# Attention and a gated dense stage on one core: from hand-ordered heads and units per batch to a task graph over 512-token chunks ordered by a list scheduler

## The chip, the cores and the metric

The kernel runs on one core of a Trainium2 chip. The metric is device time in microseconds (us) of one execution; a lower figure is better. The profile is one execution, read with the engines PE (matmul; PEld is its weight load), ACT (activation functions), DVE (vector), POOL (GpSimd, which also issues DMAs that change the type) and SP (which issues plain DMAs).

## The reference

There are 4 batches, 8 heads, 768 tokens and a head size of 64. Heads 0, 2 and 6 attend causally to everything ("retrieval" heads); the other five ("streaming" heads) attend to the first 4 tokens and to a window of 64. The 8 heads side by side make 3072 rows `x` of 512 numbers, and a gated dense stage follows.

```python
scores = scale * np.matmul(q, k.transpose(0, 1, 3, 2))
scores = np.where(mask, scores, -1e9)          # causal, or causal & (sink | window)
a = np.exp(scores - max); a = a / sum(a)
x = np.matmul(a, v)                            # -> (3072, 512)

g = x @ w_gate                                 # 512 -> 1536
gelu = 0.5 * g * (1.0 + erf(g / sqrt(2)))
val = x @ w_val                                # 512 -> 1536
ffn_out = gelu * val @ w_out                   # 1536 -> 512
res_gate = sigmoid(x @ w_res)
return x + res_gate * ffn_out
```

## The kernel before, in words

**Attention by head.** For each of the 32 (batch, head) pairs POOL issues three loads, q, k and v, each of a whole head (`qk_dma`, lines 364 and 367; `v_dma`, line 374). They turn float32 into float16 on the way. SP then transposes q and k by DMA (`qk_transposes`, lines 382 and 387) from 64 columns padded to 128, into `QT` and `KT`. Four slots (`NSLOT`) hold heads in flight. A head is worked in three pairs of 128-query tiles. A pair's scores (line 421, 256 columns per matmul) go to one of two PSUM banks; the exponential (line 438, or 433 with a bias that leaves only the sink columns) takes them to `ET`; masks are multiplied in on DVE (line 448); the product with v and a column of ones (line 463) gives 65 columns per tile, of which the last is the sum. A reciprocal (line 475) and a scaling (line 480) write `xtok` in float32.

**Dense stage by batch.** When the 8 heads of a batch are done, `x_transposes` turns `xtok` with float32 transposes on PE (line 506) and 24 copies on DVE (line 513) into `xT`. Then come 24 gate-and-value units (12 feature groups for 512 tokens, 12 for the other 256): line 550 is the gate matmul, 560 the value matmul, 569 a Tanh on ACT that stands for the error function, 573 and 577 two DVE operations that make `hT`. Six output units follow: line 597 is `hT` by `wo`, 607 `xT` by `wr`, 615 a Tanh, 619 and 624 the gating and the residual on DVE. SP stores the rows at the start of the next batch's flush (line 630).

**What sets the order.** Every engine has one queue, in program order. The main loop writes it by hand: scores of a pair, one pending dense unit, the product with v of the pair before, another dense unit. A batch's dense stage therefore lies beside the next batch's attention, batch 0's attention has no dense work beside it, and the last dense stage has no attention beside it. `flush_batch` runs between two batches. Weights are issued on POOL two chunks per head, between the loads of q, k and v (lines 292 to 306). Each task waits on the semaphores of its readers and writers (`Sched.task`).

Of the kernel before, what the change touches and what calls it, by code (L numbers as in the profile page):

```python
# [1 line left out]

# [3 lines left out]
BATCH = 4  # L7
NHEAD = 8
# [7 lines left out]

NEG = -4000.0
SM_SCALE = 1.0 / 8.0
GELU_SIG = 1.702
# [3 lines left out]

ACT_EXP = mybir.ActivationFunctionType.Exp
ACT_TANH = mybir.ActivationFunctionType.Tanh
ACT_COPY = mybir.ActivationFunctionType.Copy

ALU_MUL = mybir.AluOpType.mult
ALU_ADD = mybir.AluOpType.add
ALU_GE = mybir.AluOpType.is_ge  # L30
ALU_NE = mybir.AluOpType.not_equal


class _Token:
    __slots__ = ("sem", "val")

    def __init__(self, sem, val):
        self.sem = sem
        self.val = val


class Sched:

    ENGS = ("pe", "act", "dve", "pool", "sp")

    def __init__(self, nc):
        self.nc = nc
        self.sems = {}
        self.counts = {}
        self.prog = {e: [] for e in self.ENGS}  # L50
        self.res_writer = {}
        self.res_readers = {}
        for e in self.ENGS:
            self.sems[e] = nc.alloc_semaphore(f"cnt_{e}")
            self.counts[e] = 0
        self.dma_sems = {}
        self.dma_counts = {}

    def _collect(self, waits, reads, writes):
        for r in reads:  # L60
            w = self.res_writer.get(r)
            if w is not None:
                waits.append(w)
        for r in writes:
            w = self.res_writer.get(r)
            if w is not None:
                waits.append(w)
            for t in self.res_readers.get(r, ()):
                waits.append(t)

    def _register(self, tok, reads, writes):
        for r in reads:
            self.res_readers.setdefault(r, []).append(tok)
        for r in writes:
            self.res_writer[r] = tok
            self.res_readers[r] = []

    @staticmethod
    def _dedupe(waits):
        wd = {}  # L80
        for t in waits:
            if t is None:
                continue
            key = id(t.sem)
            cur = wd.get(key)
            if cur is None or cur[1] < t.val:
                wd[key] = (t.sem, t.val)
        return list(wd.values())

    def task(self, eng, fn, waits=(), reads=(), writes=()):  # L90
        waits = list(waits)
        self._collect(waits, reads, writes)
        wlist = self._dedupe(waits)
        self.counts[eng] += 1
        tok = _Token(self.sems[eng], self.counts[eng])
        self.prog[eng].append((fn, wlist, tok, "inst"))
        self._register(tok, reads, writes)
        return tok

    def dma(self, eng, fn, sem_name, waits=(), reads=(), writes=()):  # L100
        waits = list(waits)
        self._collect(waits, reads, writes)
        wlist = self._dedupe(waits)
        if sem_name not in self.dma_sems:
            self.dma_sems[sem_name] = self.nc.alloc_semaphore(f"dma_{sem_name}")
            self.dma_counts[sem_name] = 0
        self.dma_counts[sem_name] += 16
        tok = _Token(self.dma_sems[sem_name], self.dma_counts[sem_name])
        self.prog[eng].append((fn, wlist, tok, "dma"))
        self._register(tok, reads, writes)  # L110
        return tok

    def group_register(self, tokens, reads=(), writes=()):
        for r in reads:
            self.res_readers.setdefault(r, []).extend(tokens)
        for w in writes:
            self.res_writer[w] = tokens[-1]
            self.res_readers[w] = []

    def emit(self, eng_name, engine):  # L120
        for fn, wlist, tok, kind in self.prog[eng_name]:
            for sem, val in wlist:
                engine.wait_ge(sem, val)
            res = fn(engine)
            insts = list(res) if isinstance(res, (list, tuple)) else [res]
            last = insts[-1]
            if kind == "dma":
                last.then_inc(tok.sem, 16)
            else:
                last.then_inc(tok.sem, 1)  # L130

    def final_waits(self, engine):
        for name, sem in self.dma_sems.items():
            v = self.dma_counts[name]
            if v > 0:
                engine.wait_ge(sem, v)


def build_kernel(
    nc,  # L140
    q, k, v, moe_w_gate, moe_w_val, moe_w_out, moe_w_res, out,
    *,
    batch=BATCH, nhead=NHEAD, seq=SEQ, dhead=DHEAD,
    n_sink=N_SINK, window=WINDOW, is_retrieval=IS_RETRIEVAL,
    d_ff=D_FF,
    moe_units_per_pair=2,
    debug=None,
):
    assert dhead == 64
    d_model = nhead * dhead  # L150
    assert d_model % 128 == 0 and d_ff % 128 == 0 and seq % 128 == 0
    nt = seq // 128
    assert nt % 2 == 0
    npairs = nt // 2
    ncb = d_model // 128
    nf = d_ff // 128
    assert window == 64 and 0 < n_sink <= 4

    S = Sched(nc)

    _static_seen = set()

    def sres(*names):
        out_ = []
        for n_ in names:
            if n_ not in _static_seen:
                _static_seen.add(n_)
                out_.append(n_)
        return out_

    def sba(name, shape, dt):
        return nc.alloc_sbuf_tensor(name, list(shape), dt)

    ident32 = sba("ident32", [128, 128], FP32)
    mk_causal_l = sba("mk_causal_l", [128, 256], FP16)
    mk_causal_r = sba("mk_causal_r", [128, 256], FP16)
    mk_sink0 = sba("mk_sink0", [128, 256], FP16)
    mk_bandr = sba("mk_bandr", [128, 256], FP16)
    mk_offl = sba("mk_offl", [128, 256], FP16)
    mk_bandoff = sba("mk_bandoff", [128, 256], FP16)  # L180
    sinkbias = sba("sinkbias", [128, 1], FP32)

    NSLOT = 4
    qst = [sba(f"qst{i}", [128, nt, 128], FP16) for i in range(NSLOT)]
    kst = [sba(f"kst{i}", [128, nt, 128], FP16) for i in range(NSLOT)]
    vaug = [sba(f"vaug{i}", [128, nt, dhead + 1], FP16) for i in range(NSLOT)]
    QT = [sba(f"QT{i}", [128, seq], FP16) for i in range(NSLOT)]
    KT = [sba(f"KT{i}", [128, seq], FP16) for i in range(NSLOT)]
    ET = [sba(f"ET{i}", [128, nt * 256], FP16) for i in range(2)]
    rcp = [sba(f"rcp{i}", [128, 2], FP32) for i in range(2)]  # L190
    xtok = [sba(f"xtok{i}", [128, nt, d_model], FP32) for i in range(2)]
    xT = [sba(f"xT{i}", [128, ncb, seq], FP16) for i in range(2)]

    wg = sba("wg", [128, ncb, d_ff], FP16)
    wv = sba("wv", [128, ncb, d_ff], FP16)
    wo = sba("wo", [128, nf, d_model], FP16)
    wr = sba("wr", [128, ncb, d_model], FP16)

    ssig = [sba(f"ssig{i}", [128, 512], FP16) for i in range(2)]
    usb = [sba(f"usb{i}", [128, 512], FP16) for i in range(2)]  # L200
    hT = sba("hT", [128, nf, seq], FP16)
    srs = [sba(f"srs{i}", [128, 512], FP16) for i in range(2)]
    msb = [sba(f"msb{i}", [128, 512], FP32) for i in range(2)]
    otile = [sba(f"otile{i}", [128, 512], FP32) for i in range(2 * nt)]
    deferred_out = deque()

    PB = [nc.alloc_psum_tensor(f"pb{i}", [128, 512], FP32) for i in range(8)]
    sunit = [PB[0], PB[1]]
    pavs = [PB[2], PB[3]]
    gpss = [PB[4], PB[6]]  # L210
    vpss = [PB[5], PB[7]]
    pffs = [PB[4], PB[6]]
    prss = [PB[5], PB[7]]

    def pool_chain(res, fns):
        tok = None
        for fn in fns:
            tok = S.task("pool", fn, reads=[res], writes=[res])
        return tok

    def aff(out, op, fill, base, pattern, cm):
        return lambda e: e.affine_select(out=out, in_=out, compare_op=op, fill=fill,
                                          base=base, pattern=pattern,
                                          channel_multiplier=cm)

    def build_consts():
        pool_chain("ident32", [lambda e: e.memset(ident32[:, :], 0.0),
                               aff(ident32[:, :], ALU_NE, 1.0, 0, [[-1, 128]], 1)])
        def q0(t):
            return t[:, 0:128]  # L230

        def q1(t):
# [543 lines left out]
```

## Time and profile before

| what | value |
|---|---|
| median of 3 runs | 428.47 us (428.27, 428.47, 431.46) |
| profiled execution: span from the first to the last instruction | 427.9 us |
| profiled execution: its own time | not listed apart from the span; the span lies 0.6 us under the median of the runs |
| mean granted TensorE clock in the profile | 0.950 |
| PE busy | 341.5 us (80%), 2144 matmuls |
| DVE busy | 268.7 us (63%), 856 instructions |
| ACT busy | 166.6 us (39%), 333 instructions |
| POOL busy | 103.2 us (24%), 158 instructions |
| moved by DMA | 34.05 MB in 138471 packets; read from HBM 29.36 MB, written 6.29 MB |

How to read it: a busy share is an average over stages. PE's records overlap, because a matmul's record holds its whole way through the array, so the pitch (start to start) is what a matmul costs in a row. A table of stretches (busy time of each engine between two moments) and the chain of work that ended last (each step with what released it) show the stages apart.

### The profile page before, as it was taken

How to read it: one execution, taken by the hardware profiler on the slowest of the kernel's cores; microseconds unless marked ns; L12 is line 12 of the kernel's file. 1: busy time of each engine (PE TensorE's matmuls, PEld its weight loads, DVE VectorE, ACT ScalarE, POOL GpSimd, SP SyncE). 2: the span in 40 equal slices, each digit the busy share in tenths (PEclk: the TensorE clock that was granted, in tenths of full speed). 3: DMA queues.
4: the chain of work that ended last, by engine and by line, in shares of the span. 5: the costliest groups of instructions: out<-in, count | busy, mean ns of one | idle time of the engine just before them, and what ended most of it. 6: DMA issues, size and time to landing. Idle time of an engine off the chain costs nothing.

```text
span 427.9 us, 7653 instructions
## 1 busy us (share of the span) xinstructions
PE 341.5 (80%) x2144; PEld 189.9 (44%) x2144; DVE 268.7 (63%) x856; ACT 166.6 (39%) x333; POOL 103.2 (24%) x158
## 2 busy tenths in 40 slices
PE   0176743898987896899987896899987896899995
PEld 0043321544575443544565443444564443445742
DVE  0065533767888356767887357778886447778643
ACT  1155632145555226144555216244555215133311
POOL 9895744221224003210224022120200000000000
PEclk9999999999999999599999999599999997699999
DMA  8999999999977509925578419944551110000021
GB/s 59 158 147 126 170 163 134 119 134 105 116 95 83 51 12 89 218 40 63 49 70 89 56 9 89 207 53 51 57 57 9 51 74 27 0 2 0 2 75 74
DMA packets 138471, 34.05 MB, mean 80 GB/s; under 512 B 127168, under 2 KB 135360, under 8 KB 138432
## 3 DMA queue, kind: packets, MB, share of 16 engines
q0 software_dynamic: 83776, 14.69, 52.7%
q1 hardware_dynamic: 54656, 18.88, 28.6%
q8 instruction: 20, 0.33, 0.3%
q14 instruction: 19, 0.16, 0.1%
HBM read 29.36 MB, written 6.29 MB: 83 GB/s over the span
## 4 chain that ended last, share of the span: by engine, by line
PE 62%; DMA 10%; DVE 9%; ACT 7%; issue 6%; DVEq 0%; SPq 0%; ACTq 0%
PE pb L597 15%; PE pb L550 14%; PE pb L560 13%; PE pb L421 7%; DMA KT<-kst 6%; PE pb L463 5%; PE pb L607 5%; DMA kst<-in_k_dram 4%; DVE xT L513 4%; ACT ET L438 4%; ACT ET L433 3%; PE pb L506 2%; DVE ET L448 2%; DVE usb L573 1%; DVE xtok L480 1%
## 5 line engine op out<-in xcount | busy, mean ns | idle before, releaser
L438 ACT ACTIVATE ET<-pb 128x512 f16<-128x512 f32 (+1 forms) x172 | 91.3, 546 | 89.2 <-PE pb L421 77.1
L421 PE MATMUL pb<-QT,KT 128*128 128x256 f16 x344 | 77.0, 318 | 54.5 <-DMA KT<-kst 27.7
L550 PE MATMUL pb<-xT,wg 128*128 128x256 f16 (+1 forms) x384 | 81.3, 335 | 0.0
L569 ACT ACTIVATE ssig<-pb 128x512 f16<-128x512 f32 (+1 forms) x96 | 47.0, 490 | 83.5 <-PE pb L550 73.2
L560 PE MATMUL pb<-xT,wv 128*128 128x256 f16 (+1 forms) x384 | 78.3, 326 | 0.0
L374 POOL DMA_DIRECT2D vaug<-in_v_dram x32 | 26.7, 834 | 185.8 <-PE pb L463 77.7
L463 PE MATMUL pb<-vaug,ET 128*128 128x65 f16 x552 | 53.4, 208 | 21.6 <-DVE ET L448 8.4
L421 PEld LDWEIGHTS pb<-QT,KT 128*128 128x128 f16 x344 | 29.2, 104 | 83.5 <-issue 46.9
L597 PE MATMUL pb<-wo,hT 128*128 128x512 f16 x288 | 66.0, 379 | 0.0
L573 DVE SCALAR_TENSOR_TENSOR usb<-ssig,pb 128x512 f16<-128x512 f16 (+1 forms) x96 | 52.9, 551 | 15.4 <-ACT ssig L569 5.6
L463 PEld LDWEIGHTS pb<-vaug,ET 128*128 128x128 f16 x552 | 36.1, 105 | 49.6 <-issue 14.3
L577 DVE SCALAR_TENSOR_TENSOR hT<-usb,pb 128x512 f16<-128x512 f16 (+1 forms) x96 | 53.2, 554 | 3.3
L480 DVE TENSOR_SCALAR xtok<-pb,rcp 128x64 f32<-128x64 f32 x192 | 45.8, 280 | 10.5 <-PE pb L421 0.2
L619 DVE SCALAR_TENSOR_TENSOR msb<-srs,pb 128x512 f32<-128x512 f16 x24 | 16.5, 687 | 54.1 <-PE pb L463 26.6
L560 PEld LDWEIGHTS pb<-xT,wv 128*128 128x128 f16 x384 | 37.8, 99 | 26.3 <-issue 1.3
L550 PEld LDWEIGHTS pb<-xT,wg 128*128 128x128 f16 x384 | 35.7, 99 | 18.3 <-issue 2.2
L615 ACT ACTIVATE srs<-pb 128x512 f16<-128x512 f32 x24 | 14.3, 597 | 73.2 <-PE pb L607 64.5
L597 PEld LDWEIGHTS pb<-wo,hT 128*128 128x128 f16 x288 | 27.4, 97 | 30.0 <-DVE xtok L480 0.2
L448 DVE TENSOR_TENSOR ET<-ET,mk_causal_l 128x256 f16<-128x256 f16 x36 | 10.4, 289 | 41.0 <-POOLq L271 21.4
L364 POOL DMA_DIRECT2D qst<-in_q_dram x32 | 27.0, 845 | 30.1 <-DMA KT<-kst 30.1
L513 DVE CAST xT<-pb 128x128 f16<-128x128 f32 x96 | 26.1, 290 | 8.2 <-PE pb L506 0.4
L506 PE MATMUL pb<-ident,xtok 128*128 128x128 f32 x96 | 26.4, 434 | 5.7 <-DVE xT L513 5.3
(43 smaller groups left out, 212.9 us busy)
## 6 DMA issues: line engine op xcount, KB each, us to landing
out_dram<-otile SPq DMA_DIRECT2D x24, 256.0 KB, 2.4
qst<-in_q_dram POOLq DMA_DIRECT2D x32, 96.0 KB, 5.0
kst<-in_k_dram POOLq DMA_DIRECT2D x32, 96.0 KB, 5.3
vaug<-in_v_dram POOLq DMA_DIRECT2D x32, 96.0 KB, 3.5
wg<-in_moe_w_gate_dram POOLq DMA_DIRECT2D x6, 256.0 KB, 8.3
wv<-in_moe_w_val_dram POOLq DMA_DIRECT2D x6, 256.0 KB, 18.4
wo<-in_moe_w_out_dram POOLq DMA_DIRECT2D x4, 384.0 KB, 30.1
QT<-qst SPq DMA_TRANSPOSE x32, 3.9
```

The costliest lines, as they stand in the source:

```text
L421: return [e.matmul(bank[:, slot * 256: slot * 256 + 256], lhsT=KT[sl][:, kt * 128:(kt + 1) * 128], rhs=QT[sl][:, 256 * p:256 * p + 256], s ...
L438: exp_fn = (lambda bank=bank, r0=r0, nblk=nblk: lambda e: e.activation(out=ET[eb][:, r0 * 256:(r0 + nblk) * 256], in_=bank[:, 0:nblk * 256 ...
L463: return [e.matmul(pav[:, dq * 128: dq * 128 + dhead + 1], lhsT=ET[eb][:, rank[kt] * 256 + dq * 128: rank[kt] * 256 + dq * 128 + 128], rhs ...
L480: S.task("dve", (lambda dq=dq, qt=qt: lambda e: e.tensor_scalar(out=xtok[xb][:, qt, h * dhead:(h + 1) * dhead], in0=pav[:, dq * 128: dq * ...
L506: return [e.transpose(out=tpav[:, cb * 128:(cb + 1) * 128], in_=xtok[xb][:, tt, cb * 128:(cb + 1) * 128], identity=ident32[:, :]) for cb i ...
L513: S.task("dve", (lambda tt=tt, cb=cb, tpav=tpav: lambda e: e.tensor_copy(out=xT[xb][:, cb, tt * 128:(tt + 1) * 128], in_=tpav[:, cb * 128: ...
L550: return [e.matmul(gps[:, 0:n], lhsT=wg[:, ci, f * 128:(f + 1) * 128], rhs=xT[xb][:, ci, c0:c0 + n], start=(ci == 0), stop=(ci == ncb - 1) ...
L560: return [e.matmul(vps[:, 0:n], lhsT=wv[:, ci, f * 128:(f + 1) * 128], rhs=xT[xb][:, ci, c0:c0 + n], start=(ci == 0), stop=(ci == ncb - 1) ...
L569: S.task("act", (lambda fb=fb, gps=gps: lambda e: e.activation(out=ssig[fb][:, 0:n], in_=gps[:, 0:n], func=ACT_TANH, scale=0.5 * GELU_SIG))(),
L573: S.task("dve", (lambda fb=fb, gps=gps: lambda e: e.scalar_tensor_tensor(out=usb[fb][:, 0:n], in0=ssig[fb][:, 0:n], scalar=1.0, in1=gps[:, ...
L577: S.task("dve", (lambda fb=fb, vps=vps: lambda e: e.scalar_tensor_tensor(out=hT[:, f, c0:c0 + n], in0=usb[fb][:, 0:n], scalar=0.5, in1=vps ...
L597: return [e.matmul(pff[:, 0:d_model], lhsT=hT[:, fi, tt * 128:(tt + 1) * 128], rhs=wo[:, fi, 0:d_model], start=(fi == 0), stop=(fi == nf - 1))
```

## The change

The whole program is rewritten. `Sched`, the main loop and its helpers go; a class `Graph` takes tasks with an estimated duration, a priority, dependencies and buffers, and `schedule()` puts each engine's queue in order at build time: at every moment a free engine takes the ready task with the lowest priority number whose buffers are free. `assign_waits()` then drops the waits that follow from others.

- Tokens are cut into six chunks of 512, which cross batch borders: `CHUNKS` has (batch, first tile, last tile) segments of 2 or 4 query tiles.
- q and k of a segment are loaded for all 8 heads by one DMA each (three groups of heads in the first chunk). A partition takes `n` neighbouring tokens, so that one run is `n`*64 numbers. A DVE copy (`rp`) puts two heads side by side, PE transposes them in float16 (`qkT`), and ACT (two of the first chunk's on DVE) copies them out of PSUM (`qkE`). The DMA transposes go.
- Scores are 128 columns per block and only for blocks that the masks leave; blocks are packed up to 512 columns for one exponential. The four sink columns are copied into the previous tile's block of k and v (`ks`, `ksf`, `vs`, `vsf`), which saves the sink block of its own.
- One reciprocal and one scaling per head and segment; `x` is copied to float16 (`x16`) and transposed in float16 (`xT`).
- The Tanh and the DVE operation after it give way to one Gelu on ACT. Exponentials of chunk c wait in ACT's order until the last Gelu of chunk c-1 has run; scores of chunk c wait for the transposes of `x` of chunk c-1.
- The residual is added on POOL (on DVE in the last chunk) and each tile is stored at once by SP.

The diff, cut to its core:

```diff
+CHUNKS = (((0, 0, 4),), ((0, 4, 6), (1, 0, 2)), ((1, 2, 6),),
+          ((2, 0, 4),), ((2, 4, 6), (3, 0, 2)), ((3, 2, 6),))
...
+    P_er = Pool(many("er", 3, [128, 2304], FP16))
+    P_es = Pool(many("es", 4, [128, 1024], FP16))
+    P_av = Pool(banks[0:2])
+    P_ps = Pool(banks[2:8], caps={"moe": 4, "scr": 3})
...
+    t_causal = chain(-40, [ ... 2 operations of 512 columns ])
+    t_diag = chain(-41, [ ... 4 operations, 3 of them of 640 columns ])
+    t_prev = chain(-40, [ ... 3 operations of 512 columns ])
...
+    def load_weights():
+        for j in range(3):
+            for nm, t, src in (("g", wg, w_gate), ("v", wv, w_val)):
+                wtok[nm, j] = dma("pool", -20 + j, 3.1, ...)
+        wtok["r"] = dma("pool", -12, 3.1, ...)
+        for j in range(4):
+            wtok["o", j] = dma("pool", -11 + j, 2.3, ...)
...
+        base = {0: -60, 1: -15}.get(c, 1000 * (c - 2) + 50)
+        groups = ((0, 2), (2, 4), (4, 8)) if c == 0 else ((0, 8),)
...  # q and k: one DMA a group; v: one DMA a head for batches 0 and 1, two a batch after that
+            tt = G.add("pe", c_mm(128, 2 * n), tr, [t_ident, tokr], pr, bufs=[rp, scr], name="qkT")
+            on = "dve" if c == 0 and p % 2 == 0 else "act"
...
+                ts = G.add("pe", ..., sc, deps, pr, bufs=[scr, ...], order=chunk_xt[c - 1], name=f"sc{h}")
+                tx = G.add("act", c_act(cols), ... func=AF.Exp ..., [ts], pr, bufs=[scr, et],
+                           fset="exp", order=[last_gelu[c - 1]], name=f"exp{h}")
+                    tm = G.add("dve", c_dve(w * 128, 2, False), ... ALU.mult ..., [tx, mt], pr, name=f"mask{h}")
...
+    def gate_value(c, xtbuf, xttoks):
+        for f in range(NF):
+            pr = 1000 * c + 500 + f
+            tg = G.add("pe", c_mm(512, NCB), mk(wg, gb), xttoks + [wtok["g", f // 4]], pr, bufs=[gb, xtbuf])
+            tv = G.add("pe", c_mm(512, NCB), mk(wv, vb), xttoks + [wtok["v", f // 4]], pr, bufs=[vb, xtbuf])
+            ta = G.add("act", c_act(512), ... func=AF.Gelu ..., [tg], pr, bufs=[gb, ga], fset="gelu")
+            th = G.add("dve", c_dve(512), ... scalar_tensor_tensor(in0=gact, scalar=0.5, in1=value bank) ...)
...
+    def output(c, h, htoks, xbuf, xtoks, xtbuf, xttoks):
+        for lt in range(4):
+            pr = 1000 * c + 1600 + 10 * lt
+            tr = G.add("pe", c_mm(512, NCB), ... wr ..., name="res")
+            for j in range(4):
+                prev_t = G.add("pe", c_mm(512, 3), ... wo ..., name="ff")
+            ta = G.add("act", c_act(512), ... func=AF.Tanh, scale=0.5 ..., name="tanh")
+            t1 = G.add("dve", c_dve(512), ... (tanh + 1) * ff ..., name="gated")
+            t2 = G.add("dve" if last chunk else "pool", ..., tensor_tensor add of x, name="add")
+            dma("sp", pr, ..., name="out")
...
-    (Sched, pair_scores_exp_mask, pair_av, x_transposes, moe_units, qk_dma, v_dma, qk_transposes and the main loop)
```

Attention of chunk c has the priorities 1000c to 1000c+240, gate and value 1000c+500 and up, output 1000c+1600 and up: the output of a chunk ranks behind both the attention and the gate stage of the next one.

More of the change, by code (lines that the diff above doesn't have):

```diff
@@ new lines, with __init__, can, take @@
+class Buf:
+    __slots__ = ("pool", "kind", "slot", "left", "users", "war", "free_at")
+    def __init__(self, pool, kind=None):
+        self.pool, self.kind = pool, kind
+        self.slot = None
+        self.left = 0
+        self.users = []
+        self.war = []
+        self.free_at = 0.0
+class Pool:
+    def __init__(self, items, caps=None):
+        self.items = items
+        self.caps = caps or {}
+        self.held = {}
+        self.free = [(0.0, i) for i in range(len(items))]
+        self.last = [[] for _ in items]
+    def can(self, kind, t):
+        if kind in self.caps:
+            h = self.held.get(kind, [])
+            h[:] = [f for f in h if f is None or f > t]
+            if len(h) >= self.caps[kind]:
+                return False
+        return any(f <= t for f, _ in self.free)
+    def take(self, buf, t):
+        best = min(x for x in self.free if x[0] <= t)
+        self.free.remove(best)
+        buf.slot = best[1]
+        buf.war = list(self.last[best[1]])
+        self.held.setdefault(buf.kind, []).append(None)
+    def give(self, buf, t):
+        h = self.held[buf.kind]
+        h.remove(None)
+        h.append(t)
+        self.free.append((t, buf.slot))
+        self.last[buf.slot] = list(buf.users)
```

1204 lines of the change are left out of this document (592 added, 612 removed).

## The prediction

> **What bounds the kernel now.** I read the chain of work that ended last first, then stretches of the span between its turning points, then the groups by shape, then the timeline where a pitch was needed. The chain's rows are start, length (us), what.
>
> ```profile
> span 427.9 us, 7653 instructions
> ...
> by line: DMA KT<-kst 27.6%; DMA kst<-in_k_dram 20.8%; PE pb L421 5.9%; DVE xT L513 4.9%; PE pb L463 2.9%; issue 2.7%; PE pb L506 2.3%; PE pb L550 2.1%; ACT ET L438 2.0%; SPq L382 1.5%; DVE ET L448 1.3%; PE pb L560 1.0%; DVE xtok L480 0.6%;
> ...
> 29.43 13.20 DMA KT<-kst
> 44.15 18.72 DMA kst<-in_k_dram
> 62.94 11.60 DMA KT<-kst
> 86.87 1.68 PE pb L550 x4
> 88.55 0.86 PE pb L560 x4
> ...
> 182.40 1.70 PE pb L550 x4
> ...
> 277.70 1.71 PE pb L550 x4
> ...
> 370.52 1.51 PE pb L550 x4
> ...
> 402.56 2.59 PE pb L597 x12
> ...
> 422.42 0.88 PE pb L607 x4
> ```
>
> The row "by line" covers the first 90 us alone. Three parts follow. Up to 86.9 us DMA carries the chain (loads of k and the DMA transposes, 48% of those 90 us) and no dense matmul runs. Then come three periods of 95.5, 95.3 and 92.8 us (from the starts at 86.87, 182.40, 277.70 and 370.52), in which PE leads. From 370.5 to 423.3 the last dense stage runs alone: it holds 192 matmuls of 512 columns at 0.2155 us (2.59/12, and 0.86/4) and 96 of 256 at half of that, 51.9 us, and takes 52.8: 98%. PE can thus run almost dense.
>
> The periods can't. Busy time per stretch, with the granted clock:
>
> ```profile
> core 0: us, PE busy (x) PEld busy (x) DVE busy (x) ACT busy (x) POOL busy (x), PEclk, DMA share, GB/s
> 87.00:115.00 28.00, 26.00 (x152) 12.63 (x150) 22.01 (x55) 12.64 (x23) 6.57 (x8) 1.00 2.03 110
> ...
> 163.00:182.00 19.00, 14.31 (x88) 8.43 (x89) 15.03 (x63) 8.20 (x17) 4.93 (x6) 0.69 1.04 162
> ...
> PE pb L421 <- ACT ET L433: 19.7, 40, 0.9
> PEld pb L421 <- issue: 46.9, 74, 1.2
> ```
>
> From 163 to 182 us, between two batches, attention runs without dense work, the clock falls to 0.69 on average and the float32 transposes come. From 87 to 163 us dense and attention alternate, and PE waits at handoffs: 40 times for a biased exponential to free one of two score banks, 0.49 us each, and 74 times before a score's weight load, 0.63 us each.
>
> **The change: work on PE.** Rows for the sizes that change (mean ns of one behind the total; timeline rows are start, length, engine):
>
> ```profile
> L438 ACT ACTIVATE ET<-pb 128x512 f16<-128x512 f32 x132 | 76.2, 596 | 89.2 <-PE pb L421 77.1 <-DVE xT L513 8.9 <-PE pb L463 1.1
> L438 ACT ACTIVATE ET<-pb 128x256 f16<-128x256 f32 x40 | 15.2, 379 | 0.0
> L433 ACT ACTIVATE ET<-pb,sinkbias 128x256 f16<-128x256 f32 x40 | 19.0, 474 | 10.7 <-PE pb L421 10.0
> L569 ACT ACTIVATE ssig<-pb 128x512 f16<-128x512 f32 x48 | 28.7, 597 | 59.7 <-PE pb L550 50.1 <-DVE rcp L475 9.6
> L573 DVE SCALAR_TENSOR_TENSOR usb<-ssig,pb 128x512 f16<-128x512 f16 x48 | 33.0, 688 | 15.2 <-ACT ssig L569 5.6 <-issue 5.6 <-PE pb L550 2.5
> L480 DVE TENSOR_SCALAR xtok<-pb,rcp 128x64 f32<-128x64 f32 x192 | 45.8, 280 | 10.5 <-PE pb L421 0.2
> ...
> 119.37 0.83 PE L463 MATMUL pb<-vaug,ET 128*128 128x65 f16 x11
> 120.03 0.60 PE L550 MATMUL pb<-xT,wg 128*128 128x256 f16 x4
> 120.47 0.60 PE L560 MATMUL pb<-xT,wv 128*128 128x256 f16 x4
> ...
> 269.29 1.12 PE L506 MATMUL pb<-ident,xtok 128*128 128x128 f32 x4 [0.50 <-DVE xT L513]
> ...
> 370.10 0.42 PE L506 MATMUL pb<-ident,xtok 128*128 128x128 f32 x1
> ```
>
> Four 256-column matmuls start 0.44 us apart (120.03 to 120.47), 0.11 each; I take half, 0.056, for 128 columns. Eleven products with v take 0.66 (119.37 to 120.03), 0.06 each; short groups go at half of that, so 0.05.
> - Dense: 72 units of 8 and 24 tiles of 16 matmuls, 960 at 0.2155 = 206.9 us. The arithmetic is the same as before; only the 256-column halves become 512.
> - Scores: by the masks, 118 blocks of 128 columns a batch, 472 in all, at 0.056 = 26 us. Before: 344 at 0.11 = 38.
> - Products with v: 472 at 0.05 = 24 us (15 to 28 by the two rates). Before 552.
> - Transposes: 192 of q and k and 96 of x, in float16, at 0.056 = 16 us. The trace has only float32 ones, (1.12-0.42)/3 = 0.23 each at half clock (0.42 is one matmul's own length there). Bounds: 0.03, the short-group rate, to 0.23: 9 to 66 us. I take 0.056, as they stream 128 columns like a score block; the float32 row is the far one.
>
> Sum 273 us at full clock. Of this the first chunk's attention and gate stage are 32 us (85 blocks twice at 0.056 and 0.05, 48 transposes, 20.7 us of gate and value).
>
> **The other engines.** ACT: 132 exponentials over 60,416 columns. The two shapes of L438 give 0.848 ns per column and 162 ns fixed, so 51 + 21 = 73 us, against 110 before. Gelu is not in the trace; I take the Tanh's 597 ns at 512 columns (bounds: 379 ns, an exponential of half the size, to 1194, twice the Tanh): 72 x 0.597 = 43, output Tanh 14. The copies of q and k out of PSUM, at most 1.03 us each by the same fit, add 24. A table load is 1.28 us in the one row that the trace has, and exponential and Gelu alternate twelve times: 15 us. Together 170 us, 52% of the forecast span.
>
> ```profile
> L438 ACT ACT_TABLE_LOAD x1 | 1.3, 1283 | 0.8 <-PEq L758 0.8
> ```
>
> The Trainium skill, in "ScalarE: Activation LUTs", section "What ACT_TABLE_LOAD costs", counts 2.66 us for a switch, since a drain of 1.38 us comes on top; no run here shows a switch yet. By that the five switches that stand ahead of an attention stretch would each be 1.4 us later, up to 7 us more in the sum if PE had nothing to put there; it has 13.8 us of output matmuls per chunk there (64 at 0.2155).
>
> DVE: the product after the Tanh (L573, 33 us at 512 columns and 19.9 at 256) goes, `hT` stays at 72 x 0.69 = 50; the scaling of 192 pieces at 280 ns becomes 64 instructions of 2 or 4 pieces, 26 us at one column per 1.04 ns; the new copies (`rp`, `ks`, `vs`, the sink fixes, `x16`) are some 240, at 0.16 us fixed (280 ns less 64 columns is 213, the upper end) and a quarter to all of 1.04 ns per column 60 to 95 us. All in all 210 to 255 us against 268.7: it has room in a span over 300. It would cost time only inside an attention stretch, about 20 us of DVE beside 25 us of PE. POOL: some 70 loads at 0.85 (below), and 20 additions that wait for the gating, with the next loads queued behind them; at 0.7 to 1.4 us each (L573's length, and twice that) nobody waits, as the loads are a chunk early. The wait that could cost is new on ACT: a chunk's first exponential stands behind the last Gelu of the chunk before, and the copies of q and k and the output Tanhs are queued behind it, with PE's output banks waiting for them. Its cover is PE's output work; its price without cover is rival 1.
>
> **The start.** It is priced by itself, since neither end of it is hidden.
>
> ```profile
> L364 POOL DMA_DIRECT2D qst<-in_q_dram x32 | 27.0, 845 | 30.1 <-DMA KT<-kst 30.1
> L222 POOL TENSOR_SCALAR_AFFINE_SELECT mk_sink<-mk_sink 128x128 f16<-128x128 f16 x5 | 1.5, 295 | 0.5
> L278 POOL MEMSET qst<- 128x384 f16 x4 | 1.7, 418 | 0.3 <-POOLq L758 0.3
> ...
> DMA packets 18588, 3.56 MB, mean 119 GB/s; under 512 B 17406, under 2 KB 18587, under 8 KB 18587
> ...
> 42.67 0.61 PE L421 MATMUL pb<-QT,KT 128*128 128x256 f16 x2 [1.68 <-DMA KT<-kst]
> ...
> 120.91 0.38 PE L421 MATMUL pb<-QT,KT 128*128 128x256 f16 x2
> ```
>
> POOL first issues 14 loads at 0.85 (to about 13.5 us), then nine mask operations of up to 640 columns, about 0.6 each plus handoffs (to 20), then the six gate and value weights (to 25). The loads are 1.57 MB as written; at the 119 GB/s of the first 30 us, from 5 us on, they are there by 18. Exponentials can start near 9 and need 14 us; but masks exist only from 17 to 20, and DVE then has masks, sums, scalings and copies of eight heads, about 13 us. So the first gate matmul is at **34 us** (27 if masks weren't late; 45 if weights, 3.15 MB more, are the last at 119 GB/s). PE runs this at half clock: two score matmuls take 0.61 at 42.7 us where they take 0.38 later, though the clock row shows 1.00 there. Its 12 us become 23, and just fit. Gate and value of chunk 0 take 20.7 + 1.7 for the slow first matmuls (0.82 in 86.87's row, twice): to **56.5**.
>
> **The sum.** What is left is 273 - 32 = 241 us of PE work. The last gate and output, 34.5 us, run alone at 98%: 35.2. For the other 206 I need the share of time in which PE streams. From 87 to 163 us it was 63.4 of 76, 0.83, by these pitches (58 scores, 102 products with v, 96 and 96 gate and value, 72 and 24 output matmuls).
>
> ```profile
> L597 PE MATMUL pb<-wo,hT 128*128 128x512 f16 x72 | 16.5, 379 | 0.0
> ...
> L421 PE MATMUL pb<-QT,KT 128*128 128x256 f16 x58 | 10.6, 271 | 5.3 <-ACT ET L433 4.7 <-ACT ET L438 0.6
> L463 PE MATMUL pb<-vaug,ET 128*128 128x65 f16 x102 | 9.0, 193 | 3.0 <-PE pb L463 0.6 <-DVE ET L448 0.6
> ```
>
> The after has three score banks, no biased exponential that empties one of two, and output matmuls that any gap can take; I choose 0.90, between 0.83 and the 0.98 of the lone stage: 229 us. The tail behind the last matmul stays 427.9 - 423.3 = 4.6. 56.5 + 229 + 35.2 + 4.6 = 325.3 us of span; with the 0.6 that lie between the span before and the median, **326 us**. At 0.83 it is 345, at 0.98 307; the start moves it by -7 to +11.
>
> **The rivals.**
> 1. *Attention sets the period and the clock falls.* Exponentials of a chunk wait for the last Gelu of the one before, so attention never lies beside a gate stage, only beside output. Should ACT and DVE starve PE there, the row 163 to 182 is the model: clock 0.69. The stretch's 25 us of PE (output 13.8, the rest attention) become 36, a period 57, and the span 34 + 5 x 57 + 20.7 + 13.8 + 4.6 = **358**. For it: DVE and ACT each have about 20 us in that stretch, in a chain. Against: output work is free to fill. By the Trainium skill, "TensorE: Matmul & The Clock Gate", Part 4, transposes don't count as PE being busy, and by its Part 1 an idle window of 3.4 us halves the clock; the trace agrees as far as 0.69 goes, and each chunk here has 48 transposes.
> 2. *Handoffs make it slower.* PE takes its tasks in a fixed order built from estimated durations; a chunk has about 22 score and 32 v tasks. If each waits the 0.49 us of the L433 row, 324 x 0.49 = 159 us come on top of 303 (the sum without any loss): **462**. It decides from 0.39 us a task, where 428 is reached. Against: waits overlap with other ready tasks, and three banks let scores run ahead.
> 3. *Nearly no loss*: 0.98 and a start at 30: **303**.
> 4. *Late loads.* All loads and weights share POOL's in-order queue. If q and k of each chunk came 5 us late, PE, ACT and DVE would stop in order: 5 x 5 more, **351**. For it: loads took 32.3 us to land when weights were ahead of them. Against: they are issued a stretch of 45 us early, and the DMA transposes, 28.6% of queue time, go.
>
> ```profile
> kst<-in_k_dram POOLq DMA_DIRECT2D x3, 96.0 KB, 32.3
> q1 hardware_dynamic: 54656, 18.88, 28.6%
> ```
>
> That the change doesn't interleave at all is rival 1 without any filling.
>
> **How the numbers follow.** Forecast (310 to 345) 0.60; rival 1 0.15; rival 2 0.06; rival 3 0.10; rival 4 0.08; 0.01 for no change. 1% (4.3 us) is about what a measurement of this kernel can tell. Only rival 2 is slower, and only "no change" is within: faster 0.93, same 0.01, slower 0.06. The range 303 to 362 takes in the forecast and rivals 3, 4 and most of 1.
>
> **What would show it.** Right: the first dense matmul between 27 and 45 us; dense stretches at 1.73 us per unit (two groups of four at 0.86); PE waits per chunk of 3 to 6 us; clock near 1 from 60 us on; the chain on PE for over 70% of the span. Wrong: a clock of 0.5 to 0.7 in the stretches between gate stages (rival 1), PE waiting for ACT or DVE at most scores (rival 2), PE or ACT waiting for loads (rival 4), or a first dense matmul after 45 us.

## The result and the profile after

The changed kernel takes **333.7 us** (median; 331.9 to 335.8) where the kernel before takes 428.4 on the same chip: a ratio of 0.780 (95% interval 0.774 to 0.787). The forecast was 326 with a range of 303 to 362. The page of the changed kernel, first its span, the busy row and the chain:

```profile
span 332.6 us, 5408 instructions
...
PE 294.8 (89%) x2096; PEld 151.3 (46%) x2096; DVE 197.8 (59%) x608; ACT 178.8 (54%) x270; POOL 85.7 (26%) x102
...
PE 76%; DVE 12%; ACT 8%; DMA 1%; issue 1%; POOL 0%; DVEq 0%; POOLq 0%
PE pb L694 37%; PE pb L719 16%; PE pb L557 9%; ACT qkt L500 8%; PE pb L714 6%; PE pb L625 5%; DVE vs L464 2%; DVE rp L480 2%; PE pb L652 2%; PE pb L489 2%; DVE otile L724 1%; DVE kts L509 1%; DVE kts L513 1%; DVE x L646 1%; DMA qks<-in_k_dr
```

Before, DMA led the first 87 us and three periods of 93 to 96 us followed. Now PE holds 76% of the chain, and DMA 1%. L694 is gate and value, L719 the output by `wo`, L557 the scores. One entry doesn't belong to PE and is large: L500, ACT's copy of q and k out of PSUM, 8% or 27 us. The pieces of the chain (start, length, what) and the stretches give the stages:

```profile
37.41 18.60 PE pb L694 x80
56.27 1.35 ACT qkt L500 x2
...
59.95 1.73 PE pb L694 x8
...
98.60 9.29 ACT qkt L500 x4
...
293.84 20.89 PE pb L694 x96
...
325.96 2.60 PE pb L719 x12
```

```profile
core 0: us, PE busy (x) PEld busy (x) DVE busy (x) ACT busy (x) POOL busy (x), PEclk, DMA share, GB/s
60.00:66.00 6.00, 3.44 (x37) 2.01 (x35) 5.58 (x33) 5.55 (x10) 2.64 (x4) 1.00 1.45 181
66.00:72.00 6.00, 5.50 (x50) 3.21 (x48) 3.91 (x19) 3.73 (x8) 0.00 (x0) 0.59 1.43 186
...
102.00:108.00 6.00, 2.30 (x13) 0.90 (x12) 0.95 (x5) 6.00 (x4) 0.00 (x0) 1.00 0.88 87
108.00:114.00 6.00, 6.00 (x20) 2.29 (x21) 3.32 (x11) 1.82 (x4) 0.00 (x0) 0.72 0.00 0
```

The stages against the sum:

| stage | forecast | after | with the copies mended (first experiment) |
|---|---|---|---|
| first gate matmul at | 34 | 37.4 | 34.0 |
| gate and value of chunk 0 done at | 56.5 | 61.7 | 58.5 |
| middle, up to the last gate stage | 229 | 232.2 | 222.9 |
| last gate stage and output | 35.2 | 34.7 | 34.7 |
| behind the last matmul | 4.6 | 4.0 | 4.1 |
| span | 325.3 | 332.6 | 320.1 |

From 102 to 108 us ACT is busy all 6 us with four copies and PE works 2.3 of them; in the next stretch the granted clock is 0.72. With the copies mended (first experiment) PE is busy for all of both stretches and the clock is 1.00. From 60 to 66, at the first border of chunks, PE works 3.4 of 6 us and the clock after it is 0.59. This fall isn't the copies' doing: in the first experiment it is 0.57 from 66 to 72. In every other stretch of 6 us from 90 us on the clock is 1.00. The clock rows of the two pages (40 equal slices of the span, in tenths, 9 for 0.9 and more), first the changed kernel, then the first experiment:

```profile
PEclk9999999959999799999999999999999999999999
PEclk9999999959999999999999999999999999999999
```

### The profile page after: what moved, and what is told of

Same layout as the page of the kernel before. It is cut to its first block, busy times and chain, and to the rows that moved or that the text cites. A ratio compares the mean times of both kernels' runs of the same rounds, so it can differ in the third digit from the quotient of the medians.

```text
span 332.6 us, 5408 instructions
## 1 busy us (share of the span) xinstructions
PE 294.8 (89%) x2096; PEld 151.3 (46%) x2096; DVE 197.8 (59%) x608; ACT 178.8 (54%) x270; POOL 85.7 (26%) x102
## 4 chain that ended last, share of the span: by engine, by line
PE 76%; DVE 12%; ACT 8%; DMA 1%; issue 1%; POOL 0%; DVEq 0%; POOLq 0%
PE pb L694 37%; PE pb L719 16%; PE pb L557 9%; ACT qkt L500 8%; PE pb L714 6%; PE pb L625 5%; DVE vs L464 2%; DVE rp L480 2%; PE pb L652 2%; PE pb L489 2%; DVE otile L724 1%; DVE kts L509 1%; DVE kts L513 1%; DVE x L646 1%; DMA qks<-in_k_dram 1%; DVE xT L656 1%
## 5 line engine op out<-in xcount | busy, mean ns | idle before, releaser
L700 DVE SCALAR_TENSOR_TENSOR hT<-gact,pb 128x512 f16<-128x512 f16 x72 | 49.4, 687 | 68.1 <-PE pb L694 63.3
L698 ACT ACTIVATE gact<-pb 128x512 f16<-128x512 f32 x72 | 42.7, 599 | 81.4 <-PE pb L694 79.1
L694 PE MATMUL pb<-xT,wg 128*128 128x512 f16 x288 | 75.5, 386 | 4.6 <-DVE xT L656 3.4
L694 PE MATMUL pb<-xT,wv 128*128 128x512 f16 x288 | 75.2, 384 | 0.4 <-ACT qkt L500 0.4
L719 PE MATMUL pb<-wo,hT 128*128 128x512 f16 x288 | 73.6, 380 | 0.0
L500 ACT ACTIVATE qkt<-pb 128x512 f16<-128x512 f16 (+1 forms) x30 | 43.9, 1576 | 8.5 <-PE pb L489 8.3
L694 PEld LDWEIGHTS pb<-xT,wg 128*128 128x128 f16 x288 | 27.9, 99 | 38.9 <-DVE xT L656 3.4
L565 ACT ACTIVATE er<-pb 128x512 f16<-128x512 f32 (+2 forms) x72 | 35.2, 544 | 19.0 <-PE pb L557 18.8
L694 PEld LDWEIGHTS pb<-xT,wv 128*128 128x128 f16 x288 | 28.3, 99 | 35.2 <-issue 1.7
L565 ACT ACTIVATE es<-pb 128x512 f16<-128x512 f32 (+1 forms) x60 | 31.9, 564 | 18.6 <-PE pb L557 18.3
L557 PE MATMUL pb<-qkt 64*128 64x128 f16 (+3 forms) x276 | 34.1, 258 | 8.5 <-DVE qkt L497 4.2
L719 PEld LDWEIGHTS pb<-wo,hT 128*128 128x128 f16 x288 | 24.3, 98 | 25.2 <-issue 2.4
L399 POOL DMA_DIRECT2D va<-in_v_dram x36 | 29.4, 864 | 17.0 <-PE pb L557 17.0
L557 PEld LDWEIGHTS pb<-qkt 64*128 64x128 f16 x276 | 16.8, 101 | 21.3 <-ACT qkt L500 5.6
L714 PE MATMUL pb<-wr,xT 128*128 128x512 f16 x96 | 25.9, 394 | 0.0
```

Of the source, the lines that this page charges most:

```text
L399: return G.add(eng, issue, lambda e: e.dma_start(out_ap(), in_ap), deps, prio, bufs=bufs, dma=cost, name=name)
L500: e.activation(out=at(BB.qkt)[:, p, :, lo:hi].rearrange("c t (p j) -> c t j p", j=n), in_=at16(scr)[:, 0:2 * n * 128].rearrange("c (t j p) ...
L557: r.append(e.matmul(at(scr)[:, o:o + nq * 128], lhsT=src, rhs=at(BB.qkt)[half:half + 64, p, 0, q0 * 128:(q0 + nq) * 128], start=True, stop ...
L565: (lambda scr=scr, off=off, cols=cols, et=et: lambda e: e.activation(out=at(et)[:, off:off + cols], in_=at(scr)[:, 0:cols], func=AF.Exp, s ...
L694: return lambda e: [e.matmul(at(dst)[:, :], lhsT=w[:, ci, f * 128:(f + 1) * 128], rhs=at(xtbuf)[:, ci, :], start=(ci == 0), stop=(ci == NC ...
L698: ta = G.add("act", c_act(512), (lambda gb=gb, ga=ga: lambda e: e.activation(out=at(ga)[:, :], in_=at(gb)[:, :], func=AF.Gelu))(), [tg], p ...
```

## The experiments

**1 and 2. The copies of q and k.** The forecast took 1.03 us for 1024 columns and 0.60 for 512 (24 us in all). The groups by shape (count, busy us, mean ns):

```profile
L500 ACT ACTIVATE qkt<-pb 128x1024 f16<-128x1024 f16 x14 | 33.0, 2509 | 5.1 <-PE pb L489 5.1
L500 ACT ACTIVATE qkt<-pb 128x512 f16<-128x512 f16 x16 | 10.9, 759 | 3.3 <-PE pb L489 3.2
L497 DVE COPY qkt<-pb 128x1024 f16<-128x1024 f16 x2 | 4.9, 2426 | 1.7 <-PE pb L489 1.7
```

They are 43.9 us. The copy puts neighbouring tokens back in order as it writes: its innermost loop steps over `n` float16 numbers, 8 bytes for four tiles, 4 for two. The first experiment turns the loops so that the same copy writes in order and reads PSUM with a stride; the second leaves the reordering out (tokens are then out of order), so that both sides are in order.

```diff
-  out=at(BB.qkt)[:, p, :, lo:hi].rearrange("c t (p j) -> c t j p", j=n),
-  in_=at16(scr)[:, 0:2*n*128].rearrange("c (t j p) -> c t j p", t=2, j=n)
+  out=at(BB.qkt)[:, p, :, lo:hi].rearrange("c t (p j) -> c t p j", j=n),
+  in_=at16(scr)[:, 0:2*n*128].rearrange("c (t j p) -> c t p j", t=2, j=n)      # 1
+  out=at(BB.qkt)[:, p, :, lo:hi],  in_=at16(scr)[:, 0:2*n*128]...              # 2
```

> The copy of the transposed q and k out of PSUM walks the same elements in another order: it writes SBUF in a row and reads PSUM with a stride. Theory (the strided write of float16 is what makes 2.36 us out of the forecast 1.03 for 1024 columns, and it holds PE up at each chunk): the 1024-column copies fall to 1.0 to 1.1 us, the 512-column ones to 0.6, and the time from 333.7 to 315 to 320 us. Rival (the copy is slow because 1024 float16 columns are read from PSUM, or its length is hidden behind output matmuls): copies stay at 2 us or more, or they fall and the time stays within 3 us of 333.7.

> The same copy reads and writes in a row, so the tokens of q and k stay in the loaded order within a segment: this leaves out the reordering, only for its price. Theory: copies at 1.03 and 0.6 us, time 315 to 320, within 2 us of the version that only reads with a stride. Should a strided read of PSUM cost something too, this one is faster than that one by what the copies differ. Rival (length hidden): within 3 us of 333.7.

The first takes **322.6 us** (321.8 to 323.2; ratio 0.752, 0.748 to 0.756), the second 323.6 (0.754, 0.749 to 0.758). Groups of the first, with the rows of its chain that give the table above, and then two groups of the second:

```profile
L500 ACT ACTIVATE qkt<-pb 128x1024 f16<-128x1024 f16 x14 | 13.6, 1026 | 8.0 <-PE pb L489 7.9
L500 ACT ACTIVATE qkt<-pb 128x512 f16<-128x512 f16 x16 | 8.9, 598 | 4.3 <-PE pb L489 4.2
L497 DVE COPY qkt<-pb 128x1024 f16<-128x1024 f16 x2 | 2.4, 1217 | 1.2 <-PE pb L489 1.2
...
34.01 6.15 PE pb L694 x21
...
281.34 20.89 PE pb L694 x96
```

```profile
L500 ACT ACTIVATE qkt<-pb 128x1024 f16<-128x1024 f16 x14 | 13.6, 1026 | 7.4 <-PE pb L489 7.3
...
L497 DVE COPY qkt<-pb 128x1024 f16<-128x1024 f16 x2 | 1.4, 692 | 1.3 <-PE pb L489 1.2
```

The stride is the cost where it is written: 2509 against 1026 ns for the same columns. On the reading side it costs ACT nothing (the second's mean is 1026 and 598 as well); DVE takes 1217 ns with it and 692 without. Of the 12.5 us of span gained, 3.4 lie before the first gate matmul and 9.3 in the middle. The gain is a little under the lower end of what was expected. The first has the lowest median of all that were run.

**3. Is it the plan?** The scheduler ordered these copies by an estimate that is too short. Told the real lengths, with the same instructions:

```diff
-  evt = G.add(on, c_dve(2 * n * 128) if on == "dve" else c_act(2 * n * 128),
+  evt = G.add(on, 2.3 if n == 4 else 0.76,
```

> The instructions are those of the changed kernel; only the list scheduler is told 2.3 us (1024 columns) and 0.76 us (512) for these copies, in place of 1.04 and 0.62. Theory (the copy's own length on ACT is the cost): the time moves by at most 5 us, to 328 to 334. Rival (the plan's wrong estimate is the cost, since engines wait in a wrong order): at least two thirds of what the shorter copies bring, 322 or less.

332.1 us (331.9 to 332.9; ratio 0.774, 0.770 to 0.777). The loss is the copies' length, not the order built on a wrong estimate.

**4. One copy of 4.95 us.** Before the first gate matmul a DVE copy of `vs` takes 4.95 us where the one before it took 0.79; POOL builds the masks at the same time (timeline: start, length):

```profile
9.91 0.79 DVE L464 COPY vs<-va 128x260 f16<-128x260 f16 x1
...
11.63 4.95 DVE L464 COPY vs<-va 128x260 f16<-128x260 f16 x1
...
12.01 0.76 POOL L383 MEMSET m_diag<- 128x640 f16 x1
...
15.77 0.73 POOL L367 TENSOR_SCALAR_AFFINE_SELECT m_prev<-m_prev 128x512 f16<-128x512 f16 x1
```

The experiment lets POOL build the masks before it issues any load.

```diff
-  t_causal = chain(-40, ...)      t_diag = chain(-41, ...)      t_prev = chain(-40, ...)
+  t_causal = chain(-92, ...)      t_diag = chain(-93, ...)      t_prev = chain(-91, ...)
```

> POOL builds the masks ahead of all loads. Theory (the DVE copy of 260 columns that took 4.95 us from 11.6 to 16.6 us was shut out by POOL's memsets and selects, which ran without a gap from 12.0 to 16.4): no plain SBUF copy on DVE above 1.4 us in the first 40 us, loads 4 to 5 us later, the first gate matmul at 35 to 39 us (37.4 before), time 331 to 337. Rival (that copy waited for its data): a copy of 3 us or more stays, and the first gate matmul comes 4 us later, at 41 or more.

336.0 us (335.0 to 336.7; ratio 0.782, 0.778 to 0.786). The long copy is gone; the first load is issued 3.7 us later and the first gate matmul comes 2.8 later, at 40.2, where 35 to 39 were expected. If the later loads move the start by their whole 3.7 us, the long copy held it by 0.9. In experiment 1 that copy isn't long either (0.48 us), so the 3.4 us that it gained before the first gate matmul aren't those of the copies of q and k alone: the two of them in the chain there (2.43 us on DVE, 2.45 on ACT, against 1.22 and 1.03) make up about 2.6.

The cause of the long copy stays open. In kernel 3, whose queues are ordered otherwise, another DVE copy takes 4.38 us from 12.24 on, while POOL builds its masks from 12.06 to 18.2. In experiment 1 POOL builds them at the same time, and what stands beside them is stretched by far less (two pairs of `rp` copies at 1.47 and 1.37 us, where the first pair took 0.50).

**5. Without the interleaving.** Scores of a chunk wait for the last output matmul of the chunk before.

```diff
-  order=chunk_xt[c - 1], name=f"sc{h}")
+  order=chunk_xt[c - 1] + last_out.get(c - 1, []), name=f"sc{h}")
```

> Undoes the interleaving alone: scores of a chunk also wait, in PE's order, for the last output matmul of the chunk before; everything else is the changed kernel, planned anew. Theory (output matmuls, 13.8 us per chunk, are what fills PE while ACT and DVE work through attention): each of the five attention stretches shows PE idle for 9 us or more and a clock of 0.5 to 0.8, and the time goes to 380 to 420 us, so the interleaving is worth about half of the 95 us gained or more. Rival (the gain is the earlier start, the dropped work and the missing DMA transposes, and attention would be short anyway): 350 or less.

**383.5 us** (381.3 to 384.2; ratio 0.893, 0.888 to 0.899), 49.8 more. The stretches show where:

```profile
120.00:180.00 60.00, 55.07 (x373) 29.54 (x372) 31.22 (x99) 32.75 (x51) 9.95 (x8) 0.83 0.42 49
180.00:240.00 60.00, 51.56 (x334) 27.11 (x333) 26.76 (x77) 31.78 (x43) 5.06 (x4) 0.86 0.05 19
```

```profile
PEclk9999999995889995589997769999559999559999
```

Over these 60 us PE is busy for most of the time, at a mean clock of 0.83 to 0.86. The clock row of its page (slices of 9.5 us) shows the five attention stretches apart, with slices of 0.5 to 0.7 in each; from 144 to 156 us the clock is 0.50 while PE is busy for 11.0 of the 12 us. The falling clock came as expected, the idle time did not: PE is idle for 4.9 to 8.4 of the 30 us around each of these stretches (78 to 108, 138 to 168 and so on), under the 9 that were expected. This is rival 1 made real: attention without filling and a falling clock.

**6. Without the order of exponentials and Gelu.**

```diff
-  fset="exp", order=[last_gelu[c - 1]], name
+  fset="exp", name
```

> Takes away the rule that exponentials of a chunk wait for the last Gelu of the chunk before; by the order of ACT's queue 28 table loads stand there in place of 12. Theory (ACT has 46% of the span free, so a load costs only where PE waits for ACT): within 8 us of 333.7, table loads at 1.28 us each. Rival (each switch stops the gate stage, whose banks wait for ACT): 16 more loads at 1.3 to 2.7 us on the path, 350 to 375.

337.1 us (335.9 to 339.2; ratio 0.785, 0.780 to 0.790). ACT loads its tables 28 times in place of 12. The median is 3.4 us higher, 0.2 for each of 16 more loads, but the intervals of the two kernels overlap, so even this little is not clear of the noise. A switch in the changed kernel, Gelu to exponential (start, length):

```profile
120.46 0.60 ACT L698 ACTIVATE gact<-pb 128x512 f16<-128x512 f32 x1 [1.13 <-PE pb L694]
121.08 1.28 ACT L565 ACT_TABLE_LOAD   x1
122.37 1.57 ACT L565 ACTIVATE er<-pb 128x512 f16<-128x512 f32 x3
```

The load starts 0.02 us behind the end of the Gelu and the exponential 0.01 behind the load: a switch is 1.28 us here. The 2.66 us that the Trainium skill states in "ScalarE: Activation LUTs", section "What ACT_TABLE_LOAD costs", would have put the next piece 1.4 us later; this trace shows no such gap.

**7, 9 and 10. The waits.** `assign_waits()` drops each wait that follows from another wait of the same task or from an earlier one on that engine. The prediction's sum has no term for it. The seventh kernel puts all of them back, the ninth those of PE alone, the tenth those of the other engines; the queues' order is the same in all.

```diff
-  if not (kdma[e] >> bits[d]) & 1 and d not in dmas:
+  if d not in dmas:
...
-  if known[e].get(d.eng, -1) >= d.pos:
-      continue
...
-  if any(o is not w and o.snap[0].get(w.eng, -1) >= w.pos for o in ws + dmas):
-      continue
...
-  dmas = [d for d in dmas if not any((o.snap[1] >> bits[d]) & 1 for o in keep)]
```

> Keeps the order of all queues and puts back every wait that the planner drops because it follows from another: about 3200 instead of 410 semaphores to wait for on PE. Theory (waits that are already met cost PE nothing to speak of, and handoffs are few): 333 to 342. Rival 2 of the prediction (handoffs are what an interleaved order pays): at 0.03 us or more each PE loses 80 us or more, 415 and up, which would make the dropped waits the change's main part.

> All waits that the pruning drops are put back on TensorE alone: 3183 waits on its queue in place of 411 (1985 of the 2772 added are for DMAs that landed long ago); the other engines keep theirs. Theory: it is TensorE's queue that pays, some 0.03 us for each wait that is already met: 394 to 416 us, close to all of the 82 us of the kernel with all waits, and TensorE's gaps named 'issue'. Rival: the waits of the evicting engines and the signals behind them cost it: at most 350 us.

> The complement: all waits put back on VectorE (2354 for 623), ScalarE (733 for 277), GpSimd (209 for 36) and SyncE, TensorE keeps its 411. Theory: 333 to 350 us, since these engines are busy for 26% to 59% of the span and have room. Rival: at least 390 us, since each handoff to TensorE gets later by the waits in front of the evictions.

The number of semaphore waits in the program that was built (final waits for the stores left out), and the times:

| | waits on PE | waits on the others | us | ratio to before |
|---|---|---|---|---|
| kernel before | 1997 | 2812 | 428.4 | 1 |
| changed kernel | 411 | 960 | 333.7 | 0.780 (0.774 to 0.787) |
| 7: all put back | 3183 | 3361 | **416.0** (411.5 to 418.9) | 0.966 (0.958 to 0.975) |
| 9: PE's | 3183 | 960 | 394.0 (391.2 to 395.6) | 0.922 (0.916 to 0.929) |
| 10: the others' | 411 | 3361 | 358.5 (357.3 to 360.7) | 0.840 (0.835 to 0.845) |

My expectation for 7 (333 to 342) fell, and its rival (415 and up) held; the expectation priced a wait that is already met at next to nothing. Met they are: of the 2772 waits put back on PE, 2762 follow from something that PE has waited for earlier in its queue, and 1985 of these are for DMAs. Then 9 came in at the lower edge of its theory and 10 above its own: 60.3 us for 2772 waits on PE and 24.8 for 2401 on the others, 22 and 10 ns each. The two sum to 85 us, against 82 together. More waits also make more tasks signal: 79 more in 9, 131 more in 10. As 10 costs 24.8 us in all, signals can't be what makes up the 60.3. The profile of 9 has 6772 instructions in place of 5408, so whether a wait costs by itself or as an instruction of its own isn't told apart. The busy rows of 9 and of 7, and of 9 what PE and its weight loads waited for (us, times, longest; L626 is the product with v, L695 gate and value):

```profile
PE 325.3 (83%) x2096; PEld 165.5 (42%) x2096; DVE 196.5 (50%) x608; ACT 179.6 (46%) x270; POOL 85.7 (22%) x102
...
PE pb L626 <- issue: 18.1, 27, 0.9
PEld pb L626 <- issue: 51.8, 83, 2.8
PEld pb L695 <- issue: 12.2, 25, 2.3
```

```profile
PE 336.5 (81%) x2096; PEld 167.5 (40%) x2096; DVE 202.2 (49%) x608; ACT 180.1 (44%) x270; POOL 85.9 (21%) x102
```

In 9 PE is idle for 67.8 us against 37.8 (span less busy), 30 more, and 30.5 us busier at the same work, since its mean clock is 0.885 in place of 0.985. About half of the price is thus idle time. The largest row of it is 18.1 us ahead of the products with v, charged to "issue", where the profile shows nothing that PE waited for. The other half is a lower clock. Why the short products with v pay most isn't shown.

**8. The float32 transposes of the kernel before.** Is the clock of 0.69 at the border of batches due to them? The kernel before with `x` in float16:

```diff
-  xtok = [sba(f"xtok{i}", [128, nt, d_model], FP32) for i in range(2)]
+  xtok = [sba(f"xtok{i}", [128, nt, d_model], FP16) for i in range(2)]
```

> The kernel before, with x kept and transposed in float16 instead of float32 (the residual is added from float16 too); nothing else changes. Theory (the stretch between two batches is slow because attention and transposes lie there without dense work, with the clock down): transposes and copies get about 5 us shorter per batch, the clock still falls below 0.8 there, 408 to 422 us. Rival (the float32 transposes are what pulls the clock down and makes up the stretch): the clock stays near 1 there, 390 or less.

424.0 us (420.5 to 428.4; ratio 0.986, 0.976 to 0.995), somewhat above what was expected. The stretch from 163 to 182 us in this kernel, and its transposes below those of the kernel before:

```profile
163.00:182.00 19.00, 15.04 (x86) 7.50 (x87) 12.25 (x54) 6.69 (x13) 4.61 (x6) 0.59 1.00 164
...
L506 PE MATMUL pb<-ident,xtok 128*128 128x128 f32 x96 | 26.4, 434 | 5.7 <-DVE xT L513 5.3 <-DVE xtok L480 0.3
...
L506 PE MATMUL pb<-ident,xtok 128*128 128x128 f16 x96 | 14.6, 307 | 10.2 <-DVE xT L513 8.2 <-DVE xtok L480 2.0
```

The transposes drop from 26.4 to 14.6 us and the clock falls there all the same (0.59). So it isn't the type that makes it fall. That it is the stretch without dense work fits kernel 5, where the clock falls in each such stretch, but no run of the kernel before shows it by itself, and the transposes as such, of either type, aren't ruled out.

**11. A faster version that wasn't.** Experiment 1, and v of all batches in two transfers each, so that GpSimd reaches the masks sooner.

```diff
-  if b < 2:        # one DMA a head
+  if False:        # two DMAs a batch, as for batches 2 and 3
```

> The copies of q and k write in order and read with a stride, as in the first experiment, and the values of all three batches come with two transfers for four heads each (the kernel does that for the third batch only) in place of 24 or 16 small ones. Theory: GpSimd issues 2 in place of 8 transfers at 0.76 us before it builds the masks, VectorE's first mask multiplication comes 4 us earlier, and the first gate matmul at 29 to 31 us in place of 34.0: 317 to 321 us against 322.6. Rival: 768 KB of values lie in front of the queries or the gate weights on the queue and the start stays at 33 us or later: 322 us or more.

332.7 us (330.6 to 332.8; ratio 0.778, 0.773 to 0.783): 10 us lost, as the rival had it, and more. Its timeline and chain:

```profile
8.97 0.70 POOL L383 MEMSET m_diag<- 128x640 f16 x1
...
27.62 0.88 DVE L480 COPY rp<-qks 128x512 f16<-128x512 f16 x4
...
41.25 15.78 PE pb L694 x64
```

The masks start 3.1 us earlier (8.97 against 12.10 in experiment 1), but the `rp` copies of the last two pairs of heads stand at 27.6, against 15.4 and 16.8 there, and the first gate matmul at 41.25. DVE wasn't waiting for their loads at that moment by the trace: their place in the queue is the plan's, which counts 6.1 us of transfer for each of the two larger loads of v. What the loads alone would have cost isn't told apart from that.

**12. Both at once.** The edits of 5 and 7 together.

> Both at once: each chunk's scores wait for the last output matmul of the chunk before, and all dropped waits are put back on all engines. By themselves they cost 49.8 and 82.3 us over the 333.7 of the changed kernel. Theory: the waits cost most where PE has nothing queued in front of it, which is a stretch of attention alone, so the two add up or more: 450 to 480 us, slower than the kernel before. Rival: both take their time largely through the same falls of the clock, and it comes to 415 to 440 us, near the kernel before.

**455.8 us** (454.6 to 457.1; ratio 1.064, 1.056 to 1.073), 122.1 more than the changed kernel, against 132.1 for the two by themselves. Its busy row:

```profile
PE 342.1 (75%) x2096; PEld 174.6 (38%) x2096; DVE 197.5 (43%) x608; ACT 180.0 (40%) x270; POOL 86.5 (19%) x102
```

The same instructions, without interleaving and without the pruning of waits, are slower than the kernel before.

## Why the prediction was right, and where it wasn't

The forecast is 8 us under the time and the time lies inside the range; the sum held by its stages, for reasons of unequal worth.

- **The start** (34, measured 37.4): the step that failed is the copies' price, "at most 1.03 us each by the same fit". Two of them at 2.4 us lie on the way to the first gate matmul; with the copies mended, and the long copy of `vs` gone as well, it comes at 34.01. The bounds (27 to 45) held. The start-up matmuls ran at about half speed under a clock row of 1.00, as the prediction had read it from before: the first four of the gate take 1.87 us, the next four 1.40, and those behind them 1.03.
- **Gate and value of chunk 0** took 24.3 us where 20.7 + 1.7 were summed. The chain shows why: eight of its 96 matmuls come only at 59.95, behind transposes and copies of chunk 1 that the plan put in between.
- **The middle** (share 0.90, 229 us): 206 us of PE work in 232.2 is 0.89, so the number held, in part by luck. (The working counts 85 score blocks for the first chunk; the masks leave 65, so 2 us of work belong to the middle instead. This changes little.) It isn't the share of the design: with the copies mended it is 0.92, and with the waits put back it would have missed by far. The step from 0.83 to 0.90 was argued from score banks, biased exponentials and output matmuls that fill gaps. Of these only the filling was run by itself: it is worth 49.8 us (kernel 5). The dropped waits are worth 82.3 and had no term in the sum at all. This omission is the largest error of the working. It doesn't show in the time only because the change does drop the waits. The 0.83 also came from a kernel with 1997 waits on PE's queue, whose `Sched.task` keeps one wait per semaphore and drops none that follows from others; what they cost there no run shows.
- **Work on PE**: gate and value in 20.83 to 20.89 us a chunk (20.7), the last stage in 34.7 (35.2). Right for the dense work; scores, products with v and transposes weren't priced by themselves.

```profile
L698 ACT ACTIVATE gact<-pb 128x512 f16<-128x512 f32 x72 | 42.7, 599 | 81.4 <-PE pb L694 79.1
L565 ACT ACT_TABLE_LOAD x6 | 7.7, 1283 | 0.9 <-PEq L787 0.8
L698 ACT ACT_TABLE_LOAD x6 | 7.7, 1283 | 0.1
L728 POOL TENSOR_TENSOR otile<-otile,xtok 128x512 f32<-128x512 f32 x20 | 25.7, 1290 | 157.2 <-DVE otile L724 147.6
```

- **The other engines**: the Gelu at 599 ns (597), twelve table loads at 1283, the addition on POOL at 1.29 us (0.7 to 1.4). ACT is 178.8 us (170): the copies add 19.9 and the rest came out lower. DVE is 197.8, under the 210 to 255.
- **Rival 1** (358) didn't happen to the changed kernel, but the mechanism exists: kernel 5 is it. The changed kernel shows traces of it, a clock of 0.59 and 0.72 in two stretches; the prediction's "clock near 1 from 60 us on" was wrong there. The 0.72 goes with the copies mended, the 0.59 stays, and its cause is open.
- **Rival 2** (462, handoffs) had the right place, PE's many short tasks, with another mechanism: not a wait for another engine at 0.49 us, but the handling of waits that are already met. The pruning kept it away: without it the same queues take 416.0 us. What the third score bank adds to that was not run. Without the pruning and without the interleaving the time is 455.8, the one run that is slower than before.
- **Rival 3** (303) needed a share of 0.98 and a start at 30; they were 0.89 and 37.4.
- **Rival 4** (late loads): PE's waits come from DVE and ACT, none of weight from loads.

## What to carry to other kernels

Before the engines' work is summed, count the waits on the queue that bounds the kernel: 2772 waits that were already met cost 60 us on PE here, more than the interleaving brought. Price a copy by the stride of what it writes, not by its columns alone; here the same reordering cost ACT nothing on the reading side. An order built from estimates must be looked at again after each edit, even one that only takes instructions away.

## What was unexpected of the hardware

- A float16 write with a stride of 8 bytes takes 2509 ns for 1024 columns on ACT and 2426 on DVE, against 1026 and 692 in order; with 4 bytes it is 759 against 598 for 512. The strided read from PSUM costs ACT nothing, and DVE 1217 against 692.
- A wait that is already met cost this kernel some 22 ns on PE and 10 on the other engines, with the idle time and the lower clock that follow counted in.
- A table switch between back-to-back ACT instructions took 1.28 us, and no drain shows as a gap beside it.
- The clock was 0.50 in stretches in which PE was busy for 11.0 of 12 us with the short matmuls and transposes of attention (kernel 5).
